# A new order for the pieces of a software-pipelined attention and feed-forward kernel on one Trainium2 core

## The chip, the cores and the metric

The kernel runs on one core of one Trainium2 chip. A core has five engines with queues of their own, which run side by side and wait for each other on semaphores: TensorE (PE in the profile; PEld is its loading of weights), VectorE (DVE), ScalarE (ACT), GpSimd (POOL) and SyncE (SP). TensorE writes its results to PSUM, which has eight banks of 512 float32 columns; VectorE and ScalarE read them from there and write them to on-chip memory. Transfers to and from the chip's main memory run on 16 DMA engines; here GpSimd issues the loads and SyncE nearly all stores. The metric is the device time of one execution in microseconds (us).

## The reference

Two layers are computed, one behind the other. For each of 8 batches and 8 heads (sequence 576, head size 64, 32 memory slots):

```
a     = softmax(phi)                  # over the 32 slots
k_m   = a^T k ;  v_m = a^T v          # 32 x 64 each
attn  = softmax(q k_m^T / 8)          # 576 x 32
o     = attn v_m                      # 576 x 64
```

The outputs of the 8 heads stand side by side, which gives x with 4608 rows of 512. Then

```
h   = max(x w1, x w2, x w3)           # 4608 x 768
out = h w_out                         # 4608 x 512, float32
```

## The kernel before

**The algebra.** x is never made. Since o = attn v_m, the kernel folds v_m into the weights of each batch: wp = v_m (w1 - w3, w2 - w3), and wp3 = v_m (w3 w_out). Then the hidden layer of a batch is max(attn wp_1, attn wp_2, 0) and the output is that times w_out, plus attn wp3. All matmuls take bf16.

**The pieces.** The program is a list of 368 short words, such as `F6@2`: a letter with a number names a piece, and behind @ stands the batch. A function `issue` (line 566 and behind) turns each word into instructions in the order of the list, and no scheduler changes it: each engine gets its instructions in the order of the words, and runs them strictly in that order. So the list is at once the order of five queues. The pieces of a batch b, with the lines that the profile names:

- L0@b loads phi (L93), L1@b loads k and L2@b loads v (L97), L3@b loads q (L110). GpSimd issues them; a load for batch b waits until the buffer of batch b-2 is free.
- E@b takes the exponential of phi on ScalarE (L229).
- r0@b and r1@b copy k and v of batches 2 to 7 on GpSimd into one packed tile, `kvr` (`pack`, L103). r0 needs L1@b and r1 needs L2@b.
- B@b multiplies the exponentials by k, v and a column of ones: 72 small TensorE matmuls (L249). It needs E@b and both packs. N@b normalizes the result on VectorE (L269, L273, L283). K@b transposes it on TensorE (L298), and VectorE or ScalarE copies it out. (In batches 0 and 1 B, N and K come in two parts, as B0 and B1, and use no pack.)
- Q0@b and Q1@b transpose the halves of q on VectorE (L313).
- S@b computes the scores: 32 matmuls of 32 rows (L333) and two exponentials on ScalarE (L342), one for each of two groups g.
- For each group g, the softmax: a (transpose, L387), s (sum, L395), c (reciprocal, L404) on VectorE, m (scaling, L409) on GpSimd, X (transpose back into `attn`, L417) on VectorE. So a0, s0, c0, m0, X0 are group 0, and a1 to X1 are group 1.
- D0@b to D2@b make wp and D3@b makes wp3: eight matmuls each (L440), and a copy out of PSUM on ScalarE or VectorE.
- F0@b to F11@b make the hidden layer: four matmuls each (L466). Where the number is even the result goes through a relu (ScalarE, L170, or VectorE, L174) to a tile h1; where it is odd, VectorE takes the maximum of it and h1 (L479) into the tile hT. Every F needs both groups of `attn`.
- T0@b to T4@b make 128 rows of the output each: six matmuls with hT (L497), two with wp3 (L506; T4, which takes the last rows of two batches, has four of L515), a copy to the tile ot (L172 on ScalarE, L176 on VectorE) and a store by SyncE (L527). T needs all twelve F of its batch. T4 is there for every second batch. The last one, T3@7, comes in two halves (L538 to L559).

Further letters (Z, Y, I, W, O, V, H, M, R) occur for warming up, weights and the first batch.

**What else is in the list.** A second list holds digits: the PSUM bank that each TensorE piece writes. A piece that needs two banks takes the one of the digit and the next. A piece that writes banks must wait until the engine that reads their old contents is done. A "!" behind a word swaps ScalarE and VectorE for copying that piece's result out of PSUM; without it a table `EVAC` decides (D0, D2, D3: ScalarE, D1: VectorE; T0, T2, T4: VectorE, T1, T3: ScalarE; K: VectorE; even F: ScalarE).

Of the kernel before, what the change touches and what calls it, by code (L numbers as in the profile page):

```python
# [15 lines left out]
def kernel(  # L16
# [14 lines left out]
    B, H, S, D = q.shape  # L31
# [101 lines left out]
    for i in range(P // M):  # L133
# [4 lines left out]
    banks = iter(  # L138
        "".join(
            """  # L140
            00224460026701101401264026402640264026452063420643064206420642064562074206742064
            20642064201640264102640264026402640264072406247026402640264024602406520462046204
            62704267402640264124602416420642064206420642067676767670
            """.split()
        )
    )
# [445 lines left out]


    for w in """
        E@0 H2@0 H0@0 L3@0 Z25@0 B0@0 Y2@0 I@0 N0@0 Z2@0 K0@0! Q0@0 Q1@0 Z9@0 S@0 Z2@0 M0@0 M1@0
        R0@0 R1@0 W0@0 Y3@0 W1@0 W2@0 Z6@0 O1@0 H3@0 O3@0 O2@0 H1@0 X1@0 B1@0 X0@0 N1@0
        K1@0 O0@0 Y0@0 D1@0! D0@0! D3@0 F8@0 F10@0 F2@0 V0@0 F6@0 F0@0! Y1@0 D2@0 D4@0 F4@0
        L0@1 V1@0 F1@0 E@1 F3@0 L1@1 F5@0 F9@0 F7@0 L3@1 F11@0 B0@1 T3@0 N0@1 K0@1! L2@1 Q1@1
        L2@2 L1@2 Q0@1 L0@2 V2@0 T0@0! L3@2 S@1 T1@0 a0@1 s0@1 c0@1 m0@1 B1@1 N1@1 a1@1 L1@3
        K1@1 s1@1 D0@1 D1@1! D2@1 c1@1 m1@1 X0@1 L3@3 r1@2 X1@1 T2@0! L2@3 F6@1 F10@1 F7@1 F2@1  # L600
        F3@1 F4@1 F0@1 r0@2 E@2 F5@1 F1@1 F11@1 L0@3 L0@4 F8@1 L2@4 F9@1 B@2 D3@1 N@2 Q1@2
        T0@1! K@2 T2@1! r0@3 Q0@2 S@2 a0@2 a1@2 s1@2 c1@2 m1@2 T4@1! D1@2! s0@2 D2@2 c0@2 m0@2
        X1@2 D0@2 T3@1 Q0@3 L3@4 X0@2 Q1@3 T1@1 F0@2 F4@2 F8@2 F6@2 F9@2 E@3 F7@2 r1@3 F5@2
        F10@2 F1@2 B@3 L1@4 D3@2 N@3 L0@5 F2@2 F11@2 E@4 F3@2 L1@5 K@3 r1@4 L2@5 T2@2! S@3 T3@2
        a0@3 s0@3 c0@3 m0@3 D0@3 D2@3 a1@3 s1@3 c1@3 X0@3 D1@3! Q0@4 m1@3 T1@2 L3@5 L2@6 T0@2!
        X1@3 F10@3 r0@4 F2@3 F4@3 E@5 Q1@4 r0@5 F5@3 F3@3 L1@6 F8@3 B@4 N@4 D3@3 F9@3 F6@3
        F11@3 L0@6 K@4 F0@3 F7@3 F1@3 S@4 a0@4 T4@3! s0@4 a1@4 D0@4 c0@4 s1@4 r1@5 c1@4 D3@4
        m0@4 X0@4 Q0@5 T0@3! D1@4! D2@4 B@5 T3@3 m1@4 X1@4 L0@7 F10@4 Q1@5 N@5 F8@4 K@5 F6@4
        F9@4 S@5 F7@4 L3@6 F2@4 F4@4 a0@5 L1@7 a1@5 F0@4 s0@5 r1@6 F3@4 D0@5 r0@6 s1@5 c1@5 E@6
        D3@5 m1@5 c0@5 F1@4 T1@3 L2@7 F11@4 L3@7 E@7 F5@4 m0@5 B@6 D1@5! D2@5 X1@5 N@6 T2@3!  # L610
        X0@5 F6@5 F8@5 Q0@6 Q1@6 K@6 F4@5 F9@5 S@6 F7@5 r0@7 a0@6 F2@5 a1@6 s0@6 c0@6 F0@5
        F10@5 m0@6 F1@5 s1@6 c1@6 F11@5 F5@5 T0@4! F3@5 X0@6 T2@4! r1@7 D0@6 D1@6! Q0@7 B@7
        m1@6 N@7 X1@6 T2@5! K@7 T3@4 Q1@7 S@7 a0@7 F2@6 s0@7 a1@7 s1@7 c1@7 m1@7 c0@7 F4@6
        T4@5! D3@6 D2@7 D0@7! T0@5! D3@7 D2@6 X1@7 m0@7 D1@7! T1@4 X0@7 F6@7 F3@6 T1@5 F4@7
        F8@7 F0@7 F5@6 F10@6 F7@7 F9@7 F10@7 F5@7 F0@6 F11@7 F6@6 F1@7 F7@6 F2@7 F8@6 F11@6
        F9@6 F1@6 F3@7 T0@6! T0@7! T3@5 T2@7! T2@6! T1@6 T1@7 T3@6 T4@7! T3@7
    """.split():
        n, b = w.rstrip("!").split("@")
        issue(int(b), n, w.endswith("!"))
# [30 lines left out]
```

## Time and profile before

| what | value |
|---|---|
| median of 3 runs | 164.83 us (164.77 to 165.41) |
| profiled execution, first to last instruction | 163.3 us |
| last matmul ends | 159.60 us from the span's start |
| TensorE busy | 153.8 us |
| ScalarE, VectorE, GpSimd busy | 100.6, 90.4, 69.5 us |
| DMA | 31.77 MB in packets, mean 195 GB/s |
| mean granted clock of TensorE | 0.995 |

The profile is one execution, with times in microseconds from the span's start. Its page gives busy shares, the span in 40 slices (each digit the busy share in tenths), DMA queues, the chain of work that ended last, and groups of instructions by source line. An entry such as "POOL L103 COPY kvr<-kvo" names the engine, the line, the operation and the tiles written and read; in brackets stand the engine's idle time before it and what ended that idle time. Line numbers are those of the kernel before; behind line 592 the changed kernel's are two higher.

### The profile page before, as it was taken

How to read it: one execution, taken by the hardware profiler on the slowest of the kernel's cores; microseconds unless marked ns; L12 is line 12 of the kernel's file. 1: busy time of each engine (PE TensorE's matmuls, PEld its weight loads, DVE VectorE, ACT ScalarE, POOL GpSimd, SP SyncE). 2: the span in 40 equal slices, each digit the busy share in tenths (PEclk: the TensorE clock that was granted, in tenths of full speed). 3: DMA queues.
4: the chain of work that ended last, by engine and by line, in shares of the span. 5: the costliest groups of instructions: out<-in, count | busy, mean ns of one | idle time of the engine just before them, and what ended most of it. 6: DMA issues, size and time to landing. Idle time of an engine off the chain costs nothing.

```text
span 163.3 us, 4838 instructions
## 1 busy us (share of the span) xinstructions
PE 153.8 (94%) x2080; PEld 85.3 (52%) x2080; DVE 90.4 (55%) x181; ACT 100.6 (62%) x151; POOL 69.5 (43%) x71
## 2 busy tenths in 40 slices
PE   7978798899899999999999999999999999999990
PEld 2433444564377436743673575576553468744450
DVE  2023704798838665849399748879749128810010
ACT  4205445845497488778885899994658976223320
POOL 7932205100599259657968957646403100000000
PEclk9999999999999999999999999999999999999998
DMA  6999999999999999999999999996313130014333
GB/s 150 152 206 207 205 210 217 274 208 210 253 313 238 209 253 379 274 210 293 252 263 206 232 355 264 191 233 150 130 69 129 69 128 0 0 68 186 135 128 130
DMA packets 21974, 31.77 MB, mean 195 GB/s; under 512 B 1216, under 2 KB 16576, under 8 KB 21952
## 3 DMA queue, kind: packets, MB, share of 16 engines
q0 software_dynamic: 16080, 21.43, 68.7%
q1 hardware_dynamic: 5728, 9.90, 17.2%
q8 instruction: 16, 0.26, 0.6%
q10 hardware_dynamic: 144, 0.13, 0.2%
q14 instruction: 6, 0.05, 0.1%
HBM read 39.32 MB, written 9.44 MB: 299 GB/s over the span
## 4 chain that ended last, share of the span: by engine, by line
PE 83%; DMA 9%; POOL 2%; ACT 2%; issue 1%; DVE 1%; ACTq 0%; POOLq 0%
PE psum L497 29%; PE psum L466 28%; DMA wo_sb<-in_moe_w_out_dram 9%; PE psum L506 8%; PE psum L440 6%; PE psum L249 4%; PE psum L192 3%; PE psum L333 2%; PE psum L515 1%; ACT h L170 1%; PE psum L538 1%; PE psum L298 1%; POOL kvo L97 1%; ACT wp L172 1%; POOL qq L110 0%
## 5 line engine op out<-in xcount | busy, mean ns | idle before, releaser
L497 PE MATMUL psum<-wo_sb,hT 128*128 128x512 bf16 x210 | 51.3, 380 | 0.0
L466 PE MATMUL psum<-attn,wp 128*128 128x288 bf16 x384 | 50.5, 286 | 0.1
L479 DVE TENSOR_TENSOR hT<-psum,h 128x576 bf16<-128x576 f32 x48 | 34.2, 749 | 18.0 <-PE psum L466 12.5
L466 PEld LDWEIGHTS <-wp 128*128 128x128 bf16 x384 | 36.7, 98 | 13.2 <-issue 2.0
L172 ACT COPY ot<-psum 128x512 f32<-128x512 f32 x35 | 20.7, 591 | 32.1 <-PE psum L506 25.2
L497 PEld LDWEIGHTS <-hT 128*128 128x128 bf16 x210 | 19.2, 97 | 24.0 <-issue 4.3
L172 ACT CAST wp<-psum 128x1024 bf16<-128x1024 f32 (+1 forms) x31 | 29.2, 995 | 3.8 <-PE psum L440 2.0
L103 POOL COPY kvr<-kvo 128x2304 bf16<-128x2304 bf16 x12 | 25.3, 2111 | 13.7 <-DMA kvo<-in_k_dram 10.1
L170 ACT ACTIVATE h<-psum 128x576 bf16<-128x576 f32 x47 | 28.4, 659 | 3.5 <-PE psum L466 3.3
L409 POOL TENSOR_TENSOR t<-t,sm 128x576 bf16<-128x576 bf16 x14 | 16.1, 1154 | 24.6 <-DVE sm L404 24.4
L506 PE MATMUL psum<-wp,attn 128*128 128x512 bf16 x62 | 18.4, 379 | 0.0
L159 PE MATMUL psum<-warm 128*128 128x512 bf16 x44 | 12.1, 427 | 1.2 <-DVE warm L128 1.2
L313 DVE STREAM_TRANSPOSE qT<-qq 128x576 f32<-128x576 f32 x16 | 11.7, 747 | 1.4 <-DMA qq<-in_q_dram 1.4
L342 ACT ACTIVATE e<-psum 128x576 bf16<-128x576 f32 x16 | 9.6, 652 | 3.8 <-PE psum L333 3.8
L229 ACT ACTIVATE e<-ph 128x1152 bf16<-128x1152 f32 (+1 forms) x9 | 9.6, 1065 | 1.7 <-DMA ph<-in_phi_dram 1.6
L395 DVE TENSOR_REDUCE sm<-t 128x18 f32<-128x576 bf16 x14 | 10.3, 738 | 0.2
L387 DVE STREAM_TRANSPOSE t<-e 128x288 f32<-128x288 f32 x14 | 6.4, 465 | 6.2 <-ACT e L342 6.1
L97 POOL DMA_DIRECT2D kvo<-in_v_dram x9 | 6.7, 749 | 7.1 <-PE psum L249 4.1
L506 PEld LDWEIGHTS <-attn 128*128 128x128 bf16 x62 | 6.1, 98 | 7.1
L110 POOL DMA_DIRECT2D qq<-in_q_dram x8 | 6.2, 770 | 6.6 <-DVE h L174 3.7
L555 DVE COPY ot<-psum 128x256 f32<-128x256 f32 x1 | 0.4, 425 | 15.4 <-PE psum L546 15.4
L249 PEld LDWEIGHTS <-e 64*32 64x32 bf16 x720 | 6.9, 90 | 3.7 <-issue 3.3
(57 smaller groups left out, 114.4 us busy)
## 6 DMA issues: line engine op xcount, KB each, us to landing
out_dram<-ot SPq DMA_DIRECT2D x35, 256.0 KB, 5.6
qq<-in_q_dram POOLq DMA_DIRECT2D x8, 576.0 KB, 12.2
ph<-in_phi_dram POOLq DMA_DIRECT2D x7, 576.0 KB, 14.4
kvo<-in_k_dram POOLq DMA_DIRECT2D x7, 576.0 KB, 14.6
kvo<-in_v_dram POOLq DMA_DIRECT2D x7, 576.0 KB, 15.6
w_sb<-in_moe_w_dram POOLq DMA_DIRECT2D x3, 768.0 KB, 19.0
wo_sb<-in_moe_w_out_dram POOLq DMA_DIRECT2D x1, 768.0 KB, 14.6
ph<-in_phi_dram SPq DMA_DIRECT2D x2, 288.0 KB, 3.0
```

What stands on the lines that cost most here:

```text
L103: nc.gpsimd.tensor_copy(out=kvrs[b % 2][:, :, :, D * i : D * (i + 1)], in_=kvos[b % 2][:, 1 - i])
L159: nc.tensor.matmul(po[:, 0:BANK], lhsT=warm[:, 0:P], rhs=warm, start=True, stop=True)
L170: nc.scalar.activation(out=out_, in_=in_, func=AF.Relu)
L172: nc.scalar.copy(out=out_, in_=in_)
L249: nc.tensor.matmul(kvp[M * j : M * (j + 1), a, 0:nd], lhsT=s["e"][r, j, c, :], rhs={None: lambda: kvr[r, j, c, 0:nd], 0: lambda: k_and_one ...
L313: nc.vector.transpose(out=s["qT"][:, j].rearrange("p j c r e -> p (j c r e)").bitcast(FP32), in_=loaded[b]["q"][:, j].rearrange("p j c d - ...
L395: nc.vector.tensor_reduce(out=sm, in_=s["t", g].rearrange("p n r e -> p n e r"), op=ALU.add, axis=mybir.AxisListType.X,)
L409: nc.gpsimd.tensor_tensor(out=t, in0=t, in1=s["sm", g].unsqueeze(2).to_broadcast([P, S // HP, R, 2]), op=ALU.mult,)
L466: nc.tensor.matmul(acc[:, h, 0:SH], lhsT=wps[b][:, g, w * DF + ft * P : w * DF + (ft + 1) * P], rhs=attn[:, g, c0 : c0 + SH], start=(g == ...
L479: nc.vector.tensor_tensor(out=hT[:, ft, (b % 2) * S : (b % 2 + 1) * S].rearrange("p (h n) -> p h n", h=2), in0=a, in1=s["h1", ft], op=ALU.max,
L497: nc.tensor.matmul(po, lhsT=hT[:, fc, c0 : c0 + P], rhs=wo_sb[:, fc, :], start=(n == 0), stop=False,)
L506: nc.tensor.matmul(po, lhsT=attn[:, g, c0 : c0 + P], rhs=wp3s[b][:, g, :], start=False, stop=(g == NG - 1),)
```

## The change

The first 62 words stay as they are (up to B0@1). All words behind them are the same 306 pieces in a new order, with a new list of banks for them, and with "!" behind other words. No function is changed; sizes, loads, buffers and instructions within a piece stay as they are. By the new swaps, seven copies of T, five of D and two relus of F move from ScalarE to VectorE, and three copies of K move from VectorE to ScalarE. In the diff below, the lines of the first 62 words, which are only broken otherwise, and some lines in the middle are left out.

```
-            00224460026701101401264026402640264026452063420643064206420642064562074206742064
-            20642064201640264102640264026402640264072406247026402640264024602406520462046204
-            62704267402640264124602416420642064206420642067676767670
+            00232204420145545045024602460460246024674620540246206240264024602362070246742604
+            62064206401460642162024026402640264026401402650264264206406204602406420240260420
+            34206423426052064560242046026420640260462364204025454545
...
-        L0@1 V1@0 F1@0 E@1 F3@0 L1@1 F5@0 F9@0 F7@0 L3@1 F11@0 B0@1 T3@0 N0@1 K0@1! L2@1 Q1@1
-        L2@2 L1@2 Q0@1 L0@2 V2@0 T0@0! L3@2 S@1 T1@0 a0@1 s0@1 c0@1 m0@1 B1@1 N1@1 a1@1 L1@3
-        K1@1 s1@1 D0@1 D1@1! D2@1 c1@1 m1@1 X0@1 L3@3 r1@2 X1@1 T2@0! L2@3 F6@1 F10@1 F7@1 F2@1
-        F3@1 F4@1 F0@1 r0@2 E@2 F5@1 F1@1 F11@1 L0@3 L0@4 F8@1 L2@4 F9@1 B@2 D3@1 N@2 Q1@2
-        T0@1! K@2 T2@1! r0@3 Q0@2 S@2 a0@2 a1@2 s1@2 c1@2 m1@2 T4@1! D1@2! s0@2 D2@2 c0@2 m0@2
-        X1@2 D0@2 T3@1 Q0@3 L3@4 X0@2 Q1@3 T1@1 F0@2 F4@2 F8@2 F6@2 F9@2 E@3 F7@2 r1@3 F5@2
-        F10@2 F1@2 B@3 L1@4 D3@2 N@3 L0@5 F2@2 F11@2 E@4 F3@2 L1@5 K@3 r1@4 L2@5 T2@2! S@3 T3@2
...
+        D2@0 D4@0 F4@0 L0@1 V1@0 F1@0 E@1 F3@0 L1@1 F5@0 F9@0 F7@0 L3@1 F11@0 B0@1 N0@1
+        T0@0! Q0@1 L2@1 K0@1! Q1@1 V2@0 T3@0! L0@2 S@1 B1@1 L1@2 a0@1 N1@1 s0@1 c0@1
+        T1@0 a1@1 K1@1 L2@2 m0@1 D1@1! D0@1 s1@1 c1@1 X0@1 m1@1! X1@1 D2@1! T2@0! F10@1
+        L0@3 F8@1 F0@1! F2@1 F9@1 E@2 L3@2 F11@1 F6@1 F1@1 F4@1 r0@2 L2@3 r1@2 F7@1 F5@1
+        F3@1 B@2 N@2 D3@1 T0@1! Q1@2 K@2! T2@1! Q0@2 L1@3 S@2 a0@2 a1@2 s1@2 c1@2 T1@1!
+        E@3 s0@2 c0@2 D2@2 L3@3 m1@2! D0@2 X1@2 D1@2! T3@1 L0@4 r1@3 T4@1! D3@2 L2@4
+        L1@4 r0@3 m0@2 B@3 X0@2 F6@2 N@3 F2@2 Q1@3 F7@2 F4@2 L3@4 Q0@3 F8@2 F5@2 E@4
...
+        r1@6 F6@3 F11@3 F0@3 F7@3 K@4! F8@3 F1@3 S@4 F9@3 L3@6 B@5 a1@4 D1@4! N@5 L2@7
+        D0@4 s1@4 a0@4 Q0@5 T3@3 K@5! s0@4 T4@3! Q1@5 c0@4 D2@4! D3@4 m0@4 c1@4 D0@5
+        m1@4 X0@4 T0@3 S@5 a0@5 D3@5 X1@4 s0@5 a1@5 T1@3 c0@5 s1@5 Q0@6 L1@7 F4@4 c1@5
+        F0@4 F2@4 m1@5 m0@5! E@6 F8@4 X0@5 F1@4 T2@3! F3@4 X1@5 F6@4 F5@4 F7@4 F10@4
...
+        F6@7 F1@6 F9@6 F0@7 F5@6 F10@7 F7@7 F8@7 F11@7 T2@6! T3@6 F1@7 F4@7 F9@7 F5@7
+        T1@6 F2@7 F3@7 T0@6 T0@7! T4@7 T1@7 T2@7! T3@7
```

More of the change, by code (lines that the diff above doesn't have):

```diff
@@ L594 @@
     for w in """
-        E@0 H2@0 H0@0 L3@0 Z25@0 B0@0 Y2@0 I@0 N0@0 Z2@0 K0@0! Q0@0 Q1@0 Z9@0 S@0 Z2@0 M0@0 M1@0
-        R0@0 R1@0 W0@0 Y3@0 W1@0 W2@0 Z6@0 O1@0 H3@0 O3@0 O2@0 H1@0 X1@0 B1@0 X0@0 N1@0
-        K1@0 O0@0 Y0@0 D1@0! D0@0! D3@0 F8@0 F10@0 F2@0 V0@0 F6@0 F0@0! Y1@0 D2@0 D4@0 F4@0
-        L0@1 V1@0 F1@0 E@1 F3@0 L1@1 F5@0 F9@0 F7@0 L3@1 F11@0 B0@1 T3@0 N0@1 K0@1! L2@1 Q1@1
-        L2@2 L1@2 Q0@1 L0@2 V2@0 T0@0! L3@2 S@1 T1@0 a0@1 s0@1 c0@1 m0@1 B1@1 N1@1 a1@1 L1@3
-        K1@1 s1@1 D0@1 D1@1! D2@1 c1@1 m1@1 X0@1 L3@3 r1@2 X1@1 T2@0! L2@3 F6@1 F10@1 F7@1 F2@1
@@ L601 @@
-        F3@1 F4@1 F0@1 r0@2 E@2 F5@1 F1@1 F11@1 L0@3 L0@4 F8@1 L2@4 F9@1 B@2 D3@1 N@2 Q1@2
-        T0@1! K@2 T2@1! r0@3 Q0@2 S@2 a0@2 a1@2 s1@2 c1@2 m1@2 T4@1! D1@2! s0@2 D2@2 c0@2 m0@2
-        X1@2 D0@2 T3@1 Q0@3 L3@4 X0@2 Q1@3 T1@1 F0@2 F4@2 F8@2 F6@2 F9@2 E@3 F7@2 r1@3 F5@2
-        F10@2 F1@2 B@3 L1@4 D3@2 N@3 L0@5 F2@2 F11@2 E@4 F3@2 L1@5 K@3 r1@4 L2@5 T2@2! S@3 T3@2
-        a0@3 s0@3 c0@3 m0@3 D0@3 D2@3 a1@3 s1@3 c1@3 X0@3 D1@3! Q0@4 m1@3 T1@2 L3@5 L2@6 T0@2!
-        X1@3 F10@3 r0@4 F2@3 F4@3 E@5 Q1@4 r0@5 F5@3 F3@3 L1@6 F8@3 B@4 N@4 D3@3 F9@3 F6@3
@@ L607 @@
[L607 to L616, printed above, removed]
+        E@0 H2@0 H0@0 L3@0 Z25@0 B0@0 Y2@0 I@0 N0@0 Z2@0 K0@0! Q0@0 Q1@0 Z9@0 S@0 Z2@0
+        M0@0 M1@0 R0@0 R1@0 W0@0 Y3@0 W1@0 W2@0 Z6@0 O1@0 H3@0 O3@0 O2@0 H1@0 X1@0 B1@0
@@ new lines @@
+        X0@0 N1@0 K1@0 O0@0 Y0@0 D1@0! D0@0! D3@0 F8@0 F10@0 F2@0 V0@0 F6@0 F0@0! Y1@0
+        D2@0 D4@0 F4@0 L0@1 V1@0 F1@0 E@1 F3@0 L1@1 F5@0 F9@0 F7@0 L3@1 F11@0 B0@1 N0@1
[3 more added lines that the diff above has]
+        F3@1 B@2 N@2 D3@1 T0@1! Q1@2 K@2! T2@1! Q0@2 L1@3 S@2 a0@2 a1@2 s1@2 c1@2 T1@1!
@@ new lines @@
+        E@3 s0@2 c0@2 D2@2 L3@3 m1@2! D0@2 X1@2 D1@2! T3@1 L0@4 r1@3 T4@1! D3@2 L2@4
+        L1@4 r0@3 m0@2 B@3 X0@2 F6@2 N@3 F2@2 Q1@3 F7@2 F4@2 L3@4 Q0@3 F8@2 F5@2 E@4
+        L0@5 F9@2 F0@2 F3@2 F10@2 F1@2 L2@5 F11@2 L1@5 L3@5 r1@4 K@3 T2@2 S@3 a0@3 s0@3
+        c0@3 a1@3 T1@2 D0@3 L2@6 D1@3! r0@4 s1@3 D3@3! c1@3 Q0@4 T0@2! L0@6 B@4 m0@3
+        D2@3 X0@3 T3@2 m1@3 X1@3 r1@5 F4@3 N@4 r0@5 Q1@4 F2@3 L1@6 F10@3 F5@3 E@5 F3@3
+        r1@6 F6@3 F11@3 F0@3 F7@3 K@4! F8@3 F1@3 S@4 F9@3 L3@6 B@5 a1@4 D1@4! N@5 L2@7
@@ new lines @@
+        D0@4 s1@4 a0@4 Q0@5 T3@3 K@5! s0@4 T4@3! Q1@5 c0@4 D2@4! D3@4 m0@4 c1@4 D0@5
+        m1@4 X0@4 T0@3 S@5 a0@5 D3@5 X1@4 s0@5 a1@5 T1@3 c0@5 s1@5 Q0@6 L1@7 F4@4 c1@5
+        F0@4 F2@4 m1@5 m0@5! E@6 F8@4 X0@5 F1@4 T2@3! F3@4 X1@5 F6@4 F5@4 F7@4 F10@4
+        L3@7 F6@5 F9@4 F4@5 F11@4 r0@6 F2@5 L0@7 F0@5 B@6 D2@5 D1@5 T0@4! N@6 F10@5 F3@5
+        F8@5 E@7 r1@7 F11@5 F7@5 Q1@6 F9@5 F5@5 T1@4 F1@5 K@6 T4@5 S@6 r0@7 Q1@7 B@7 N@7
+        D0@6 a1@6 Q0@7 T2@5! s1@6 K@7 a0@6 c1@6 m1@6 T3@5 s0@6 D1@6 S@7 a1@7 c0@6 T3@4
@@ L617 @@
+        s1@7 D0@7 D2@7 m0@6! D3@6 X0@6 T1@5 T0@5! D3@7 a0@7 s0@7 c1@7 X1@6 c0@7 D1@7!
+        D2@6! T2@4! m0@7 m1@7! F10@6! F6@6 F7@6 F0@6 F11@6 X1@7 F2@6 F4@6 F8@6 X0@7 F3@6
+        F6@7 F1@6 F9@6 F0@7 F5@6 F10@7 F7@7 F8@7 F11@7 T2@6! T3@6 F1@7 F4@7 F9@7 F5@7
+        T1@6 F2@7 F3@7 T0@6 T0@7! T4@7 T1@7 T2@7! T3@7
     """.split():
```

## The prediction

> **What bounds the kernel now.** I read the busy shares first, then the slices with the granted clock, then the chain that ended last, then GpSimd's timeline, because the packs and the attention scaling share that queue.
>
> ```profile
> PE 153.8 (94%) x2080; PEld 85.3 (52%) x2080; DVE 90.4 (55%) x181; ACT 100.6 (62%) x151; POOL 69.5 (43%) x71
> PE   7978798899899999999999999999999999999990
> PE psum L497 29%; PE psum L466 28%; DMA wo_sb<-in_moe_w_out_dram 9%; PE psum L506 8%; PE psum L440 6%; PE psum L249 4%; PE psum L192 3%; PE psum L333 2%; PE psum L515 1%; ACT h L170 1%; PE psum L538 1%; PE psum L298 1%; POOL kvo L97 1%; ACT wp L172 1%; POOL qq L110 0%
> ```
>
> TensorE is busy 94% of the span, and the chain that ended last is TensorE from 24 us on except for a few short links. The last wait worth naming is in batch 1, in the chain in order of time:
>
> ```profile
> 41.80 0.73 PE psum L249 x72
> 42.53 0.02 issue
> 42.56 0.29 DVE kvn L273
> 42.85 0.38 DVE t L387
> 43.23 0.17 DVE kvt L176
> 43.41 0.04 issue
> 43.45 0.84 PE psum L440 x24
> ```
>
> B1@1 at 41.7 is followed by DVE, by K1@1, by DVE, by D0@1, with nothing to run in between: 0.9 us. From there to the last matmul's end at 159.60 TensorE never stands still for long. So the new order can win little, and loses whatever it makes TensorE wait. GpSimd's timeline shows what could make it wait:
>
> ```profile
> 56.34 2.11 POOL L103 COPY kvr<-kvo 128x2304 bf16<-128x2304 bf16 x1 [2.90 <-DMA kvo<-in_k_dram]
> 60.10 2.27 POOL L409 TENSOR_TENSOR t<-t,sm 128x576 bf16<-128x576 bf16 x2 [1.65 <-DVE sm L404]
> 62.33 0.79 POOL L110 DMA_DIRECT2D qq<-in_q_dram  x1
> 63.51 2.11 POOL L103 COPY kvr<-kvo 128x2304 bf16<-128x2304 bf16 x1 [0.39 <-DMA kvo<-in_v_dram]
> 65.56 0.74 POOL L97 DMA_DIRECT2D kvo<-in_k_dram  x1
> ```
>
> A pack holds GpSimd 2.11 us, a scaling 1.15, a DMA issue 0.75, one behind the other. Here r0@3 is through before batch 2's scalings, and r1@3 follows them; nine F@2 pieces (4.57 us from 63.23) keep TensorE busy until B@3 at 67.73.
>
> **The change part by part.** *TensorE's own work* is the same 2080 matmuls. In the trace a piece's pitch to the next is steady: F 0.490 us, T 1.727 (T4 1.94), K 0.167, D 0.216, B about 0.58. Entering B, D or S from F or T costs 0.093; leaving D costs 0.116 and 0.010 more. Behind the common pieces the old order has 22 such groups and the new one 19, but four times S now stands beside B or D, a pair the trace doesn't show. If a junction is free the gain is 3 x 0.23 = 0.69; if it costs a whole group change, 0.23 is lost. I take the middle, -0.33, since S alone (0.41 for 32 matmuls) already seems to pay its own filling. [...] No row of before shows such a pair.
>
> *Waits removed.* Pitches without any wait lay the old order from 35.03 to 158.47; the trace has 159.60. So the old waits are 1.13 us (0.42 and 0.48 in batch 1, the rest in pieces under 0.15): -1.13. With the new order the same sum ends at 158.14.
>
> *Batches 1 and 2.* B1@1 is now due at 39.87, but L2@1 lands at 40.53 (issued 19.92, 20.6 to landing): +0.7. T1@0 now covers N1@1, but K1@1 still runs straight into D1@1: +0.48 as before. Then B@2. The old order queues L2@2, L1@2, L0@2, and the last lands at 50.0 (26.79 + 23.2). The new one queues L0@2, L1@2, L2@2: same bytes, so the last lands at 50.0 too, but now it is V, and its pack takes 2.11. B@2 can start at 52.3 and would be due at 50.91: **+1.39** in all, the two earlier waits inside it.
>
> *GpSimd's queue in batches 2 and 3*, the main term. The new order on GpSimd is m1@2, L0@4, r1@3, L2@4, L1@4, r0@3, m0@2; on TensorE, B@3 and F6@2 now stand ahead of every F@2. S@2 starts at 52.3 + 4.69 (B@2 with D3@1 0.96, T0@1 1.74, K@2 0.17, T2@1 1.82) = 56.95. In the trace m1@2 begins 3.47 after S@2 (56.63 to 60.10), behind the same a0, a1, s1, c1: 60.42. Then m1@2 1.13, L0@4 0.75, r1@3 2.07, two issues 1.50, r0@3 2.11: 67.98, and B@3 starts at 68.03. TensorE has only S@2 0.41, T1@1 1.83, three D 0.77, T3@1 1.74, T4@1 2.04, D3@2 0.22 to run, 7.01, and is due at 63.96: it stands 4.07. m0@2 runs to 69.09, X0@2 (0.48) to 69.60, F6@2 starts at 69.65, where B@3's 0.76 would have let it start at 68.79: 0.86 more. Together **+4.93**. L1@3 isn't what holds r0@3: the old order's four transfers after 50.0 come 2.8 to 4.4 apart, so the new fourth, one of them the small phi, lands by 62.5, and GpSimd arrives at 65.9. DVE stands at X0@2 meanwhile with N@3 queued behind it, and K@3 follows late but under the twelve F@2.
>
> *Batch 5.* DVE now takes X0@5 ahead of F1@4's maximum, and F6@4 writes the banks (0 and 1) that F1@4 filled. From S@5: a0@5 can start 1.19 later; a0, X1@4, s0, a1, c0, s1, Q0@6, c1 are 4.19 by their rows, less 0.08 of overlap at each, 3.55; m1@5 and m0@5 on GpSimd 2.4; X0@5 0.47, the maximum 0.67, 0.05 to TensorE: 8.35. TensorE's pieces from S@5 to F6@4 are 7.15: **+1.20**. Two small waits, T4@3 and D0@6: +0.2.
>
> *Engines of evacuations.* Seven T, five D and two F relus move to DVE, three K to ScalarE. DVE: 7 x 0.70 (between 0.425 for 256 columns and 1.225 for 1024) + 5 x 1.225 + 2 x 0.758 - 3 x 0.358 = +11.5, to 102 us; ScalarE falls to about 91.5. Neither comes near TensorE's load. T1@1's copy delays c0@2 by 0.6, hidden since m0@2 waits for r0@3, six us later; without that cover it would cost 0.6. SP's 35 stores keep their count, and the last pieces still end in T3@7: 0. Loads issued later by GpSimd still have over 4 us of queued transfers ahead of them (L3@4 issued at 69.1, L1@4 landing at 74), and the last landing, 114.6 in the trace, is needed after 122: 0, unless the queue runs dry.
>
> *The clock.* TensorE's last matmul ends at 159.60 and the granted clock falls to half at 161.70, 2.10 us later:
>
> ```profile
> 160.00:161.00 1.00, 0.00 (x0) 0.00 (x0) 0.00 (x0) 0.04 (x1) 0.00 (x0) 1.00 0.43 144
> 161.00:162.00 1.00, 0.00 (x0) 0.00 (x0) 0.00 (x0) 0.00 (x0) 0.00 (x0) 0.85 0.35 118
> ```
>
> The warm-up matmuls run at 0.427 apart for the first 3.5 us and at 0.216 behind. A stand of four us before B@3 is longer than 2.10, so I expect half clock from there until 3.5 us after work returns: to 71.5 counted from B@3, to 73.15 from F6@2. F@2 pieces lose half of that, 0.95 or 1.75; ends 0 and 1.75, I take **+1.3**. [...]
>
> **Sum.** -0.33 - 1.13 + 1.39 + 4.93 + 1.20 + 0.2 + 1.3 = +7.56. The profiled execution spans 163.3 us with 3.7 behind the last matmul, which stay; the median of the runs is 164.83, 1.5 above that span. 164.83 + 7.56 = 172.4.
>
> **The rivals.** *The clock stays up* (chance 0.22): all the waits as above, 171.1. For it: no gap in the middle of the trace ever dropped the clock, though the longest there was 1 us. *The waits are shorter* (0.08): F6@4's is hidden, or GpSimd gets to r0@3 a little earlier, and the clock stays: 169.0 to 170.5. *A landing becomes the bound* (0.09): stores slow the loads so that r0@3 waits for L1@3 past 65.9, or L2@6 comes too late for r1@6; each us late is a us, 174 to 176. Against it: margins of 3 us and more. *TensorE stays covered, not slower* (0.06): it decides whether the chain from S@2 to F6@2, 12.7 by the rows, is in fact no longer than the 7.8 of TensorE work beside it, which it is if packs and DMA issues let the next GpSimd instruction start while they run. Then only batch 1 and 2 and the junctions remain: 164.83 - 0.33 - 1.13 + 1.39 = 164.8, or 164.2 with free junctions. Against it: at 63.51 and 65.56 the issue begins where the pack ends.
>
> **How the numbers follow.** The forecast with its clock loss has 0.55, 171.4 to 174.6, likeliest 172.4. From the low case 169.0 to 174.6 holds a little over 8 in 10. Under 0.5% this kernel's measurement can't tell a change (its three runs differ by 0.4%). Slower 0.94 (the first four cases), same 0.04 and faster 0.02 from the last.
>
> **What would show it.** In the changed profile: TensorE idle about 4 us before B@3 (L249) with the pack (L103) as releaser, and about 1 us before F6@2 (L466) with DVE's L417; GpSimd without a gap from m1@2 to m0@2; a clock digit under 9 behind it; F matmuls about 0.24 apart there; 1.2 us before F6@4 released by L479; an order without waits 0.3 shorter. I am wrong if GpSimd shows m0@2 done by 65, if B@2 starts before 51.5, or if DMA releases the packs.

## The result and the profile after

The changed kernel takes 172.82 us (median of 4 executions, 172.58 to 173.34) against 164.91 us (4 executions, 164.77 to 165.41) for the kernel before on the same chip: a ratio of 1.0458, 95% interval 1.0394 to 1.0521 (the two medians divide to 1.048, inside that interval). It is 7.9 us slower, where 172.4 (169.0 to 174.6) was forecast. Its profiled execution took 172.69 us with a span of 170.9; the last matmul ends at 167.17 instead of 159.60, and the 3.7 us behind it are the same. The ratios here and below leave out executions more than 1.5% above the fastest of their kernel, of which fill_gap has one and both_loads two, while the medians count every execution.

From the page of the changed kernel: busy time, TensorE's 40 slices, the granted clock, the chain's shares by engine, and the group of B's matmuls.

```profile
PE 156.2 (91%) x2080; PEld 86.8 (51%) x2080; DVE 100.6 (59%) x192; ACT 93.7 (55%) x140; POOL 69.3 (41%) x71
PE   7986799999999991899999999799999999999991
PEclk9999999999999997599999999999999999999999
PE 66%; POOL 13%; DMA 9%; issue 6%; ACT 2%; DVE 2%; POOLq 0%; ACTq 0%; DVEq 0%
L249 PE MATMUL psum<-kvr,e 64*32 64x129 bf16 x432 | 5.2, 237 | 4.0 <-POOL kvr L103 4.0
```

TensorE has a hole in one slice (the digit 1), and the clock is at 7 tenths in that slice and at 5 in the next. GpSimd's share of the chain is now 13%; the same line of the kernel before has 2%:

```profile
PE 83%; DMA 9%; POOL 2%; ACT 2%; issue 1%; DVE 1%; ACTq 0%; POOLq 0%
```

All of B's idle time, 4.0 us, was ended by a pack (L103). GpSimd's timeline at that place, in columns start, duration, operation, idle time before it:

```profile
60.17 1.15 POOL L409 TENSOR_TENSOR t<-t,sm 128x576 bf16<-128x576 bf16 x1 [6.80 <-DVE sm L404]
61.28 0.81 POOL L93 DMA_DIRECT2D ph<-in_phi_dram  x1
62.08 2.12 POOL L103 COPY kvr<-kvo 128x2304 bf16<-128x2304 bf16 x1
64.13 0.75 POOL L97 DMA_DIRECT2D kvo<-in_v_dram  x1
64.87 0.75 POOL L97 DMA_DIRECT2D kvo<-in_k_dram  x1
65.60 2.12 POOL L103 COPY kvr<-kvo 128x2304 bf16<-128x2304 bf16 x1
67.67 1.17 POOL L409 TENSOR_TENSOR t<-t,sm 128x576 bf16<-128x576 bf16 x1
```

These are m1@2, L0@4, r1@3, L2@4, L1@4, r0@3, m0@2, one behind the other without a gap: 7.5 us from m1@2's start to m0@2's. TensorE in the same stretch:

```profile
63.40 0.41 PE L440 MATMUL psum<-w3o,kvt 64*32 64x512 bf16 x8
67.78 1.18 PE L249 MATMUL psum<-kvr,e 64*32 64x129 bf16 x72 [3.96 <-POOL kvr L103]
69.41 2.82 PE L466 MATMUL psum<-attn,wp 128*128 128x288 bf16 x11 [0.46 <-DVE rden L269]
```

D3@2 is through at 63.8, B@3 starts at 67.78, when r0@3 is through, and F6@2 at 69.41, when m0@2 and X0@2 are. In 2-us stretches (columns: stretch, length, busy time of PE, PEld, DVE, ACT and POOL, granted clock, DMA share, GB/s):

```profile
64.00:66.00 2.00, 0.00 (x0) 0.00 (x0) 0.00 (x0) 1.06 (x2) 2.00 (x4) 1.00 1.04 361
66.00:68.00 2.00, 0.22 (x24) 0.22 (x31) 0.00 (x0) 0.00 (x0) 2.00 (x2) 0.59 1.07 332
68.00:70.00 2.00, 1.54 (x75) 1.10 (x59) 1.09 (x5) 0.00 (x0) 2.00 (x3) 0.50 1.21 214
70.00:72.00 2.00, 2.00 (x10) 1.19 (x9) 0.93 (x2) 1.10 (x2) 1.81 (x3) 0.50 1.21 208
72.00:74.00 2.00, 2.00 (x13) 1.38 (x12) 1.42 (x2) 0.79 (x3) 0.00 (x0) 0.70 1.21 206
```

From 64 to 66 only ScalarE and GpSimd work. The clock falls at 66.36 and is back at 73.18, and in that time the four pieces F6@2, F2@2, F7@2 and F4@2 follow each other by 0.94 to 0.96 us, where an F takes 0.49. The wait of batch 5, on TensorE and on VectorE:

```profile
107.65 0.65 PE L466 MATMUL psum<-attn,wp 128*128 128x288 bf16 x4
109.28 2.00 PE L466 MATMUL psum<-attn,wp 128*128 128x288 bf16 x15 [0.98 <-DVE hT L479]
```

```profile
108.11 0.48 DVE L417 STREAM_TRANSPOSE attn<-t 128x288 f32<-128x288 f32 x1 [2.39 <-POOL t L409]
108.51 1.38 DVE L479 TENSOR_TENSOR hT<-psum,h 128x576 bf16<-128x576 f32 x2
```

VectorE stands 2.39 us for X0@5 (L417), whose input m0@5 is late, and only then takes the maxima of F1@4 and F3@4 (L479); the first of the two sets F6@4's banks free.

**Where the 7.57 us came from.** Each number is the distance from the start of a piece's first matmul to that of the next, less the distance of the same pair where nothing waits (F 0.49, T 1.73, D 0.22 and so on). Predicted first, then measured:

| term | predicted | measured |
|---|---|---|
| the order without waits | -0.33 | -0.2 |
| old waits gone | -1.13 | -1.45 |
| batches 1 and 2 (before B1@1, D1@1, B@2) | +1.39 | 0.30 + 0.47 + 0.10 = +0.87 |
| before B@3 and F6@2 | 4.07 + 0.86 = +4.93 | 4.15 + 0.87 = +5.02 |
| half clock | +1.3 | +1.83 |
| before F6@4 | +1.20 | +1.14 |
| small waits | +0.2 | +0.16 |
| B0@1 starts later in this execution | 0 | +0.23 |
| sum | +7.56 | +7.6 |

How the first two rows are divided depends on which distance is taken as free of waits; together they are -1.46 predicted and -1.65 measured.

### The profile page after: what moved, and what is told of

Same layout as the page of the kernel before. It is cut to its first block, busy times and chain, and to the rows that moved or that the text cites. A ratio compares the mean times of both kernels' runs of the same rounds, so it can differ in the third digit from the quotient of the medians.

```text
span 170.9 us, 4840 instructions
## 1 busy us (share of the span) xinstructions
PE 156.2 (91%) x2080; PEld 86.8 (51%) x2080; DVE 100.6 (59%) x192; ACT 93.7 (55%) x140; POOL 69.3 (41%) x71
## 4 chain that ended last, share of the span: by engine, by line
PE 66%; POOL 13%; DMA 9%; issue 6%; ACT 2%; DVE 2%; POOLq 0%; ACTq 0%; DVEq 0%
PE psum L466 24%; PE psum L497 22%; DMA wo_sb<-in_moe_w_out_dram 9%; PE psum L506 6%; POOL kvr L103 5%; PE psum L440 4%; PE psum L192 3%; POOL t L409 3%; PE psum L249 3%; POOL kvo L97 2%; PE psum L333 2%; POOL qq L110 1%; ACT h L170 1%; PE psum L515 1%; PE psum L538 1%
## 5 line engine op out<-in xcount | busy, mean ns | idle before, releaser
L466 PE MATMUL psum<-attn,wp 128*128 128x288 bf16 x384 | 51.4, 292 | 1.5 <-DVE hT L479 1.0
L466 PEld LDWEIGHTS <-wp 128*128 128x128 bf16 x384 | 37.9, 100 | 14.9 <-issue 1.8
L479 DVE TENSOR_TENSOR hT<-psum,h 128x576 bf16<-128x576 f32 x48 | 34.6, 752 | 14.5 <-PE psum L466 11.8
L170 ACT ACTIVATE h<-psum 128x576 bf16<-128x576 f32 x45 | 27.9, 652 | 14.3 <-PE psum L466 14.0
L172 ACT COPY ot<-psum 128x512 f32<-128x512 f32 x28 | 16.5, 588 | 29.5 <-PE psum L506 26.0
L172 ACT CAST wp<-psum 128x1024 bf16<-128x1024 f32 (+1 forms) x26 | 24.7, 988 | 3.3 <-PE psum L440 2.9
L103 POOL COPY kvr<-kvo 128x2304 bf16<-128x2304 bf16 x12 | 25.3, 2116 | 3.0 <-PE psum L466 3.0
L417 DVE STREAM_TRANSPOSE attn<-t 128x288 f32<-128x288 f32 x14 | 6.2, 450 | 11.2 <-POOL t L409 11.2
L176 DVE CAST wp<-psum 128x1024 bf16<-128x1024 f32 x7 | 8.5, 1218 | 5.1 <-PE psum L440 5.1
L249 PE MATMUL psum<-kvr,e 64*32 64x129 bf16 x432 | 5.2, 237 | 4.0 <-POOL kvr L103 4.0
```

What stands on the lines that cost most here:

```text
L103: nc.gpsimd.tensor_copy(out=kvrs[b % 2][:, :, :, D * i : D * (i + 1)], in_=kvos[b % 2][:, 1 - i])
L170: nc.scalar.activation(out=out_, in_=in_, func=AF.Relu)
L172: nc.scalar.copy(out=out_, in_=in_)
L249: nc.tensor.matmul(kvp[M * j : M * (j + 1), a, 0:nd], lhsT=s["e"][r, j, c, :], rhs={None: lambda: kvr[r, j, c, 0:nd], 0: lambda: k_and_one ...
L466: nc.tensor.matmul(acc[:, h, 0:SH], lhsT=wps[b][:, g, w * DF + ft * P : w * DF + (ft + 1) * P], rhs=attn[:, g, c0 : c0 + SH], start=(g == ...
L479: nc.vector.tensor_tensor(out=hT[:, ft, (b % 2) * S : (b % 2 + 1) * S].rearrange("p (h n) -> p h n", h=2), in0=a, in1=s["h1", ft], op=ALU.max,
```

## The experiments

In all, twelve kernels were run, each beside the kernel before on the same chip. Where a text below gives a landing or the start of a piece without a fence, it counts from the start of the span; several of the expectations count from a point 0.24 us later. The waits before B1@1 and B@2 end on landings and vary from one execution to the next: in the profiles of the new order they come to 0.3 to 1.45 us together, where none of the edits below but old_swaps has had any effect yet. So a difference of less than about 1 us between two kernels is read here from the waits and not from the time.

| kernel | us, median | ratio to before, 95% |
|---|---|---|
| changed kernel | 172.82 | 1.0394 to 1.0521 |
| before_r1_first | 171.18 | 1.0338 to 1.0464 |
| before_r1_fill | 169.31 | 1.0164 to 1.0279 |
| m0_early | 173.56 | 1.0496 to 1.0551 |
| b3_late | 175.12 | 1.0555 to 1.0653 |
| both | 174.64 | 1.0538 to 1.0605 |
| both_half | 168.78 | 1.0191 to 1.0260 |
| after_half | 173.58 | 1.0443 to 1.0549 |
| both_loads | 174.44 | 1.0347 to 1.0551 |
| fill_gap | 172.70 | 1.0414 to 1.0504 |
| fill_half | 171.30 | 1.0286 to 1.0388 |
| x0_late | 171.46 | 1.0353 to 1.0417 |
| old_swaps | 175.64 | 1.0553 to 1.0652 |

### One pack ahead of a scaling, in the kernel before

```
-  s0@2 D2@2 c0@2 m0@2 X1@2 ... E@3 F7@2 r1@3 F5@2
+  s0@2 D2@2 c0@2 r1@3 m0@2 X1@2 ... E@3 F7@2 F5@2
```

> The kernel before with one move: r1@3 ahead of m0@2 on GpSimd's queue, directly behind c0@2, as the new order has a pack ahead of m0@2. There m0@2 ran from 60.1 to 62.4 us (with m1@2's end), and r1@3 waited for its landing until 63.27 us and ended at 65.37. Theory A (a pack ahead of m0@2 costs what TensorE then waits for at the first piece that reads X0@2's transposes, and the kernel before has nothing later that stands to swallow it): m0@2 ends near 66.5 us, F0@2 starts 3.8 to 4.1 us later, and with 0 to 1.8 us of half clock the time is 164.9 + 3.9 + 0.9 = 169.7 us, between 168.5 and 171.0. Rival B (the stand is given back later, out of waits that the kernel before has on landings): below 167 us.

Measured: 171.18 us, 6.0 more than the 165.15 of the kernel before beside it. GpSimd, then TensorE, of this kernel:

```profile
59.89 1.15 POOL L409 TENSOR_TENSOR t<-t,sm 128x576 bf16<-128x576 bf16 x1 [1.41 <-DVE sm L404]
63.52 2.10 POOL L103 COPY kvr<-kvo 128x2304 bf16<-128x2304 bf16 x1 [2.49 <-DMA kvo<-in_v_dram]
65.59 1.15 POOL L409 TENSOR_TENSOR t<-t,sm 128x576 bf16<-128x576 bf16 x1
```

```profile
62.58 0.59 PE L506 MATMUL psum<-wp,attn 128*128 128x512 bf16 x2
67.30 5.92 PE L466 MATMUL psum<-attn,wp 128*128 128x288 bf16 x34 [4.13 <-DVE attn L417]
```

The pack waits 2.49 us for its landing with m0@2 queued behind it, and TensorE stands 4.13 us before F0@2. The four pieces behind lose 1.59 us to the half clock. The last matmul ends 5.7 us later than before, where the stand and the clock come to 5.9: next to nothing is given back. Theory A holds, and the time is 0.2 above its range, since the half clock took more than the 0.9 allowed for. One move of one word on GpSimd's queue makes a loss three quarters the size of that of the whole new order.

### The half clock as a cost of its own

The stand of that kernel was filled with 17 matmuls that no output needs (the word Z17@0, and a digit for it in the list of banks):

```
-  X0@2 Q1@3 T1@1 F0@2 F4@2
+  X0@2 Q1@3 T1@1 Z17@0 F0@2 F4@2
```

> The kernel with r1@3 ahead of m0@2 in the old order (171.2 us; TensorE stood 4.29 us before F0@2 and lost 1.59 us to the half clock in the four pieces behind it), plus 17 matmuls that no output needs in F0@2's bank between T1@1 and F0@2. Theory A (the half clock is a cost of its own, which the stand brings and work in the stand avoids): the granted clock stays at 1.00 and the time is 171.2 - 1.6 = 169.6 us, between 169.1 and 170.2. Rival B (what the clock gives is taken back by the next landing, as it seemed where the stand of the changed kernel was filled): 170.8 to 171.5 us.

Measured: 169.31 us, 1.9 less than without the filling (2.9 by the two ratios; the last matmul of the profiled executions ends 1.5 earlier). The granted clock by slices, and TensorE, of this kernel:

```profile
PEclk9999999999999999999999999999999999999998
```

```profile
63.59 3.83 PE L159 MATMUL psum<-warm 128*128 128x512 bf16 x17
67.57 4.57 PE L466 MATMUL psum<-attn,wp 128*128 128x288 bf16 x36
```

The 36 matmuls of nine F take 4.57 us again, as in the kernel before, though F0@2 starts no earlier than without the filling. Theory A holds: the clock is a term of its own. In the changed kernel the same filling had come out otherwise:

```
-  T4@1! D3@2 L2@4
+  T4@1! D3@2 Z17@0 L2@4
```

> The changed kernel with 17 extra dummy matmuls (17 x 0.216 = 3.7 us, into banks that nobody reads then) between D3@2 and B@3, so that TensorE is busy while it waits for the pack. They add work that no output needs. If the slow F@2 pieces of the changed kernel (0.94 to 0.96 us each instead of 0.49, four of them, 1.83 us) are due to the clock that fell in the stand, the clock stays at 1.00, the four pieces take 0.49, and the time falls from 172.8 to 171.0, while B@3 and F6@2 start where they did. If VectorE or ScalarE made them slow, nothing changes: 172.8. If TensorE's 4 us in front of B@3 were TensorE's own limit, the dummies add 3.7: 176.5.

Measured: 172.70 us, a ratio of 1.0459 and so no gain, and the expectation was missed. The clock stayed at 1.00 and F followed F by 0.49, so 1.83 us were won there. But F6@4 waited 1.56 instead of 1.14, a small wait of 0.16 came at T0@3, and in this execution B1@1 waited 0.39 more, for a landing that came 0.77 later, with B0@1 itself 0.38 later. The last two lie ahead of everything that was changed. In the two profiled executions these terms add up to -0.48 us, and the last matmul does end 0.48 earlier. The longer wait before F6@4 is one for a landing: the chain that leads to it goes back to Q0@6 on VectorE, which stands 0.33 us for q of batch 6 (landed at 104.27) ahead of c1@5 and so of m1@5 and m0@5. So the loads were suspected, and the loads of k and v of batches 4 to 7 were halved on top of the filling (the edit is shown under "Is it the input stream?"):

> The changed kernel with 17 matmuls that no output needs in the stand before B@3, and with the loads of k and v for batches 4 to 7 cut to half their columns (outputs of those batches are not the reference's). With whole loads the filled stand kept the clock at 1.00 and yet gave 172.7 us, as the changed kernel; with half loads and no filling the time was 173.6 us, 2.2 us of it in five pieces at half clock. Theory A (the landings took the clock's gain back): 173.6 - 2.0 = 171.6 us, between 170.8 and 172.2. Rival B (the filling itself, or the start of the program, took it): 172.5 to 173.7 us.

Measured: 171.30 us, 1.4 less than fill_gap and 2.3 less than after_half, its counterpart without the filling, in whose profile five F pieces lost 2.2 us to the half clock. Theory A holds in sign and size: with room in the transfers, filling the stand wins what the clock costs, and the wait before F6@4 is back to 1.14. How fill_gap's missing gain divides in the executions that were not profiled isn't known.

### Taking the stand away

m0@2 was put ahead of the packs, so that it runs directly behind m1@2:

```
-  L3@3 m1@2! D0@2 ... L1@4 r0@3 m0@2 B@3
+  L3@3 m1@2! m0@2 D0@2 ... L1@4 r0@3 B@3
```

> The changed kernel with one word moved: m0@2 directly behind m1@2, ahead of L0@4, r1@3, L2@4, L1@4 and r0@3 on GpSimd. Theory (GpSimd's queue, and B@3 standing ahead of the F@2 on TensorE): attn of batch 2 is ready at 63.3, but B@3 is in front of F6@2 and its pack r0@3 now ends 1.5 later (67.7 to 69.2); F6@2 then waits no more for X0@2, which had cost 0.87. Net 0.6 to 1.4 slower than the changed kernel: 173.4 to 174.2. Rival (the late m0@2 alone is the cause): about 5 us and the clock come back, 166.

Measured: 173.56 us, as expected, though partly by chance. The wait before B@3 grew to 5.64, since m0@2 and its own wait now lie ahead of both packs, and that before F6@2 shrank to 0.35. The queue's length is what counts, not which of its members stands last. But the half clock cost only 0.9 us here, which cancels the net growth of the two waits, and the 1.0 us by which the last matmul ends later in the profiled execution lies ahead of the move: the waits before B1@1 and B@2 are 1.45 instead of 0.40.

Then B@3 and N@3 were put behind nine F@2 (and five bank digits changed so that no piece waits for B@3's banks):

```
-  r0@3 m0@2 B@3 X0@2 F6@2 N@3 F2@2 ... F0@2 F3@2
+  r0@3 m0@2 X0@2 F6@2 F2@2 ... F0@2 B@3 N@3 F3@2
```

> The changed kernel with B@3 and N@3 moved behind nine of the twelve F@2, as they stand in the kernel before (the banks of five pieces behind it changed to suit); m0@2 stays behind r0@3 on GpSimd. Theory: F6@2 now waits for X0@2 until 69.4, as it did, so the stand is 5.6 us in one, and B@3 no longer runs inside it: about 0.6 slower than the changed kernel, 173.0 to 174.0. Rival (B@3's place on TensorE alone is the cause): about 5 us and the clock come back, 166.

Measured: 175.12 us, over a microsecond above the expectation. Now F6@2 stands 5.65, for m0@2 behind the same packs; six F run slow (2.6 us); and N@3 and K@3 have too few F left above them, so that T2@2 waits 0.91 and F11@2 0.37. A move of TensorE's words doesn't help while GpSimd's are where they are, and it costs cover elsewhere.

So both moves were made together, with r0@3 directly behind r1@3:

```
-  L3@3 m1@2! D0@2 ... r1@3 T4@1! D3@2 L2@4 L1@4 r0@3 m0@2 B@3 X0@2 F6@2 N@3 F2@2 ... F0@2 F3@2
+  L3@3 m1@2! m0@2 D0@2 ... r1@3 r0@3 T4@1! D3@2 L2@4 L1@4 X0@2 F6@2 F2@2 ... F0@2 B@3 N@3 F3@2
```

> Both moves together, and r0@3 directly behind r1@3, ahead of L2@4 and L1@4. Theory: m0@2 is done at 62.9, X0@2 at 63.4, so F6@2 starts when D3@2 is through (63.6); r0@3 is done by 68.0, about when nine F@2 are through. The two waits (4.15 and 0.87) and the clock loss (1.83) go: 172.8 - 6.85 = 166.0, between 165.5 and 166.8. Rival (landings of batch 3's k and v hold B@3): B@3 still stands several us behind the nine F@2, 168 or more.

Measured: 174.64 us, 8.6 above the expectation. The two waits are gone: F6@2 follows D3@2 at once, with 0.4 us of small waits behind it, and the clock stays up there. But TensorE and GpSimd later show (TensorE first):

```profile
89.34 0.66 PE L466 MATMUL psum<-attn,wp 128*128 128x288 bf16 x4
93.32 1.03 PE L249 MATMUL psum<-kvr,e 64*32 64x129 bf16 x72 [3.32 <-POOL kvr L103]
```

```profile
87.68 2.11 POOL L103 COPY kvr<-kvo 128x2304 bf16<-128x2304 bf16 x1 [4.72 <-DMA kvo<-in_v_dram]
91.16 2.11 POOL L103 COPY kvr<-kvo 128x2304 bf16<-128x2304 bf16 x1 [1.38 <-DMA kvo<-in_k_dram]
```

Behind both packs of batch 5 stands the arrival of their data. B@5 starts at 93.3, which is where the changed kernel has it (93.35): the whole gain is lost again. The clock falls once more (1.5 us), F6@4 waits 1.83, and the waits before F1@2 and T2@2 come to 1.8 (in b3_late those before F11@2 and T2@2 come to 1.3). In the changed kernel L1@5 lands at 85.6, in this one at 91.1, because L2@4 and L1@4 now go out at 68.4 and 69.2, behind r0@3, where the changed kernel sends them at 64.1 and 64.9; whether the later issue is the reason is tried last in the next group. An arrival also stands behind the wait before F6@4: the chain to it goes back to q of batch 6, landed at 106.94, for which Q0@6 waits on VectorE.

### Is it the input stream?

In both kernels the loads of k and v for batches 4 to 7 were cut to half their columns:

```
     def load_kv(b, i, h=slice(0, NP)):
         kv = loaded.setdefault(b, {})["kv"] = kvos[b % 2]
+        if b >= 4:
+            h = halves[0]
```

> The kernel with m0@2 early, B@3 late and r0@3 directly behind r1@3 (174.6 us), and with the loads of k and v for batches 4 to 7 cut to half their columns (outputs of those batches are not the reference's). There the two waits of the prediction at B@3 and F6@2 were gone, and TensorE stood 3.39 us before B@5, whose pack waited for a landing at 90.87 us, lost about 1.5 us to the half clock behind it, and stood 1.83 us before F6@4. Theory A (the input stream is a second bound, just under the stand; without it the gain that the prediction's sum gives to the removed waits appears): the 3.39 and the 1.5 go, 1.83 stays within 1, so 174.6 - 4.9 = 169.7 us, between 168.5 and 170.5. Rival B (the wait before B@5 is one of GpSimd's queue or of TensorE's order and not of the bytes): 174.0 to 175.0 us as before.

> The changed kernel with its loads of k and v for batches 4 to 7 cut to half their columns (half the bytes; the packs copy what lies there, so the outputs of those batches are not the reference's). It tells whether the input stream bounds the new order as it stands. Theory A (under the stand before B@3 the transfers have slack: B@5 starts at 93.1 us, 3.6 us after its second pack, and no wait of more than 0.1 us in the table of this kernel ends on a landing behind batch 2): 172.6 us, between 172.0 and 173.2, with the wait before B@3 still near 4.1 us. Rival B (the landings set the pace of the new order in batches 4 to 7 already): faster by 1 us or more, below 171.7 us.

Measured: both_half 168.78 us, 5.9 less than with whole loads; after_half 173.58, no less than with whole loads. The clock by slices and TensorE of both_half (its lines are numbered two higher):

```profile
PEclk9999999999999999999999999999999999999999
```

```profile
88.70 0.67 PE L468 MATMUL psum<-attn,wp 128*128 128x288 bf16 x4
89.30 0.80 PE L251 MATMUL psum<-kvr,e 64*32 64x129 bf16 x72
```

B@5 now follows its predecessor without a wait, the clock stays up, and F6@4 is back to 1.14. Theory A holds for both_half, in time and in waits. For after_half it holds in the waits, and the time is 0.4 above the expected range: the wait before B@3 is 4.1, none of TensorE's waits behind it ends on a pack, but the waits before B1@1 and B@2, ahead of every halved load, are 1.4 instead of 0.4 in the profiled execution, and the half clock cost 2.2. Without the stand, the arrival of the inputs is the bound, and in the changed kernel it is hidden under the stand. Neither the removal of the stand alone (+1.8 us) nor the smaller loads alone (+0.8) wins anything; together they win 4.0. The prediction's sum has 6.85 for the stand and the clock; in the profile of both_half new waits of 0.3 before F2@2, 1.0 before F1@2 and 1.1 before T2@2 take 2.4 of it back. The one before F1@2 is an arrival as well, of phi, which was not halved: ScalarE stands 1.62 us for it with E@4, ahead of the relu of F10@2 (1.36 in both).

Last, the two loads were sent ahead of r0@3 again:

```
-  r1@3 r0@3 T4@1! D3@2 L2@4 L1@4 X0@2
+  r1@3 T4@1! D3@2 L2@4 L1@4 r0@3 X0@2
```

> The kernel with m0@2 early and B@3 late (174.6 us), but with r0@3 left behind the loads L2@4 and L1@4, as in the changed kernel, so that these two loads go out about 3 us earlier. Halving the later loads there took the time to 168.8 us, since the wait before B@5 (3.39 us, for L1@5 at 90.87) and the half clock behind it went. Theory A (the landing of L1@5 is the bound, and a load that goes out earlier lands earlier): L1@5 lands near 88.5 us, the wait before B@5 falls to 0.8 to 1.4 us, the clock stays up there, and the time is 174.6 - 2.3 - 1.4 = 170.9 us, between 170.0 and 172.3. Rival B (the bytes alone decide, not the time of issue, as the transfers never paused): 174.0 to 175.0 us.

Measured: 174.44 us, but four executions from 172.1 to 175.6, so this run doesn't decide between the theories. In the one that was profiled, the fastest, L1@5 lands at 88.4 and B@5 waits 0.71 with the clock at full, which is what theory A says of this place. The time went elsewhere: B@3 waits 1.07, F0@4 0.66 and F6@4 2.69, the last two behind r1@6, which starts at 95.0, when its data have landed at 94.9. Queued behind it on GpSimd are L3@6 and m0@4. The chain to F6@4 goes over L3@6: it goes out at 97.05, q of batch 6 lands at 104.20, and Q0@6 stands 0.87 us for it on VectorE, ahead of c1@5 and so of m1@5 and m0@5. It is the pattern of batch 3 over again, with a load between. VectorE at this place, Q0@6 and c1@5:

```profile
104.22 0.78 DVE L313 STREAM_TRANSPOSE qT<-qq 128x576 f32<-128x576 f32 x1 [0.87 <-DMA qq<-in_q_dram]
104.93 0.22 DVE L404 RECIPROCAL sm<-sm 128x18 f32<-128x18 f32 x1
```

The other executions had a lower mean clock (0.988 to 0.990 instead of 0.996); what they waited for isn't known.

### Batch 5 and the choice of engines

```
-  E@6 F8@4 X0@5 F1@4 T2@3! F3@4 X1@5 F6@4
+  E@6 F8@4 F1@4 T2@3! F3@4 X0@5 X1@5 F6@4
```

> The changed kernel with X0@5 moved behind F3@4 in the list, so that VectorE takes F1@4's and F3@4's maxima ahead of it. Theory A (the prediction's term for batch 5: VectorE stands for X0@5's product while the banks that F6@4 needs wait for the maxima behind it): the 1.14 us before F6@4 go, 172.8 - 1.1 = 171.7 us, between 171.3 and 172.2. Rival B (another stand follows, at F6@5 or B@6, and takes the gain back, as it did in the runs that took away the stand before B@3): 172.5 to 173.1 us.

Measured: 171.46 us, 1.4 less than the changed kernel (1.2 by the two ratios). TensorE, then VectorE, of this kernel:

```profile
107.19 5.57 PE L466 MATMUL psum<-attn,wp 128*128 128x288 bf16 x44
```

```profile
107.95 0.76 DVE L479 TENSOR_TENSOR hT<-psum,h 128x576 bf16<-128x576 f32 x1 [1.46 <-PE psum L466]
108.63 0.83 DVE L417 STREAM_TRANSPOSE attn<-t 128x288 f32<-128x288 f32 x2
```

The maximum of F3@4 comes ahead of X0@5, and eleven F run on end. Theory A holds. (In this execution, at a mean clock of 0.990, the half clock also lasted only 3.4 us and cost 1.0 instead of 1.83; the other three, whose mean clock was 0.976, took 171.34 to 171.70.)

Finally, the changed kernel with the old "!" on every word, so that only order and banks are new:

```
-  K@2! ... T1@1! ... m1@4 X0@4 T0@3 S@5 a0@5 D3@5
+  K@2 ... T1@1 ... m1@4 X0@4 T0@3! S@5 a0@5 D3@5
...
```

> The changed kernel's order and banks with the choice of ScalarE or VectorE for each piece as in the kernel before. The prediction gave the choices, with the order on a piece's own path, 0.33 us of gain in all, and said that VectorE's 10 us of additional work lie beside TensorE's. Theory A (that work is covered): 172.8 us, between 172.2 and 173.6. Rival B (VectorE's greater load holds TensorE up): below 171.8 us.

Measured: 175.64 us, 2.8 more than the changed kernel (2.4 by the two ratios); both theories were wrong. ScalarE, then TensorE, of this kernel late in the program:

```profile
139.50 2.85 ACT L172 CAST wp<-psum 128x1024 bf16<-128x1024 f32 x3
142.21 0.63 ACT L172 COPY ot<-psum 128x512 f32<-128x512 f32 x1
```

```profile
142.40 4.82 PE L466 MATMUL psum<-attn,wp 128*128 128x288 bf16 x38 [0.86 <-ACT wp L172]
```

With the old choices ScalarE has three wide copies on end, and F10@6 waits for the last of them, 1.03 us by the distance of the pieces. There are more of this kind: 0.60 in the F of batch 1, 0.48 before D3@5, 0.34 before D2@3, 0.18 more before F6@4, and three of 0.11 to 0.13. ScalarE is busy 101.1 us, 58% of the span, so the share doesn't show it.

## Why the prediction was right

*What bounds it.* That TensorE had no slack and that the new order loses whatever TensorE waits for was right: 7.57 us later by the last matmul, 7.9 by the medians. That the sum of +7.56 meets the 7.57 so closely is luck: the parts in batches 1 and 2 and the old waits are off by -0.5 and -0.3, and the clock, the order without waits and a later B0@1, which no term had, by +0.5, +0.1 and +0.2. The main term, by itself two thirds of the sum, isn't luck.

*GpSimd's queue in batches 2 and 3.* Right to 0.1 us, and by the same steps: m1@2 at 60.17 (60.42 predicted; 52.3 + 4.69 there is 56.99 and not 56.95, which moves nothing), B@3 at 67.78 (68.03), F6@2 at 69.41 (69.65). before_r1_first shows by itself that a pack ahead of a scaling is dear, in the old order too. The claim that L1@3 doesn't hold r0@3 was also right: r0@3 starts where the issue ahead of it ends.

*Batches 1 and 2.* The mechanism was right, the size off by 0.5: "the last lands at 50.0" failed. In the profiled execution L2@2 landed at 49.7 and its pack ended at 51.96, so that B@2 waited 0.10. Across the runs of this order that landing lies between 49.7 and 50.8, and the wait before B@2 between 0 and 0.75. The wait before B1@1 was 0.30, not 0.7: TensorE came 0.3 later to it and the landing 0.1 earlier.

*The order without waits.* -0.2 where -0.33 was written down. The middle of -0.69 and +0.23, which the prediction meant to take, is -0.23, and its whole sum would have been +7.66; in the same way 164.2 in its last rival should be 164.4. The piece behind an S starts 0.41 to 0.43 after it where nothing else waits, whether that is a B, a D, an F or a T, so no cost of its own shows on leaving S; but leaving D for S costs 0.12 (0.339 from D1@6 to S@7, where D follows D by 0.216), much as leaving D for F or T. So the trace lies about midway between a whole group change at each junction (+0.23) and free ones (-0.69).

*Batch 5.* Right: 1.14 for 1.20, and x0_late takes it away.

*The clock.* It fell, as the likeliest case had it, and cost 1.83 for the 1.3 taken from ends of 0 and 1.75. The step "half clock until 3.5 us after work returns" is right in size and wrong in kind (below). What happened is its upper end (half clock to 73.15 forecast, to 73.18 measured), and that end was met by luck, since what a stand costs doesn't follow its length (below). Rival "the clock stays up" is out: in all profiled kernels with an unfilled stand of 4 us or more the clock fell (mean granted clock 0.978 to 0.990).

*Engines of evacuations.* "0" was right for the kernel as it stands, and the reason too weak. The sum of busy time is not what makes the choices free: old_swaps has the same order, less work on VectorE, and is 2.8 us slower. The choices belong to the order.

*A landing becomes the bound.* Not in the changed kernel, but the margin named there, "over 4 us of queued transfers", was no margin for a faster order: both and both_half show a second bound at B@5, just under the stand, and in fill_gap, both and both_loads the landing of q of batch 6 lengthens the wait before F6@4. The prediction's sum is right as a sum of what is there; it is not a list of what could be won back. Of the 5.0 + 1.8 us of waits and clock around B@3, the order "both" won nothing.

None of the runs of the new order is faster than the kernel before; the best with the full computation is x0_late at 171.46.

## What to carry to other kernels

On an engine that runs strictly in order, price a moved step by everything queued behind it up to the next thing that the bounding engine reads: here one pack ahead of one scaling cost 6 us, made up of 2.1 of its own, 2.5 of its wait for data and 1.6 of half clock. When a wait is taken away and nothing is won, look for the same engine standing later at another source (here the arrival of inputs) before giving up the first cause, and make the suspected source smaller to see it. Busy shares of 55 to 60% say nothing about whether copies may be shifted between two engines; the wait before each piece does.

## What was not expected of the hardware

The clock doesn't fall a fixed time after the last matmul, nor come back a fixed time after the first. It fell 2.1 us after the last matmul's end at the end of the kernel before (159.60, 161.70), 2.5 before B@3 in the changed kernel (63.82, 66.36) and 5.0 at that kernel's end (167.17, 172.17). In the kernel "both" it fell when work had already returned, at 93.5, 0.2 us behind the first matmul of B@5 (granted clock 0.85 from 90 to 95 us); in x0_late it fell during B@3, whose 72 matmuls took 1.02 us there, against 0.80 at full clock in fill_gap and 1.18 at half clock in the changed kernel. It was back 5.4 us after B@3's first matmul in the changed kernel and 3.7 after B@5's in "both" (0.80 from 95 to 100 us).

Nor does the price follow the length of the stand: m0_early lost 0.9 us with a stand of 5.64 (mean clock 0.990, which makes 3.4 us at half clock), the changed kernel 1.8 with one of 4.15 (0.980, and 6.83 us at half clock), and the four executions of m0_early had mean clocks from 0.969 to 0.990. The kernel before ran 157.01 us at full clock from the warm-up to its fall; the changed kernel 61.44 to its first fall, then 6.83 at half clock and 98.99 at full clock to the next fall. The three stretches at full clock are 46, 18 and 29 times 3.413 us, and the 6.83 is twice that. In the last 3.41 us before the three falls TensorE had 1.30 us of matmuls (the kernel before), 0.87 and none (the changed kernel). Of the 6.83 at half clock in the changed kernel, the first half had 1.54 us of matmuls and the second had them throughout. How much work it takes to keep the clock up or to bring it back isn't shown by these.
